# Attention scores of a pooled-attention and gated-MLP kernel: from one 128-row product for two heads to 64-row products for single heads, in turns on the two halves of TensorE

## The chip, the cores and the metric

The kernel runs on one core of a Trainium2 chip. The metric is the device time of one execution in microseconds (us). The median of three runs before the change is 771.92 us.

## What is computed

Pooled attention over 8 batches, 8 heads, 576 tokens and head size 64, and behind it a gated two-matrix product with two more matrices. All inputs are float32.

```python
k_p = k.reshape(B, H, Sp, pool, D).mean(axis=3)      # 576 keys -> 72 pooled keys
v_p = v.reshape(B, H, Sp, pool, D).mean(axis=3)
scores = scale * np.matmul(q, k_p.transpose(0, 1, 3, 2))
scores = scores - np.max(scores, axis=-1, keepdims=True)
attn = np.exp(scores)
attn = attn / (np.sum(attn, axis=-1, keepdims=True) + 1e-09)
attn_out = np.matmul(attn, v_p)
x = attn_out.transpose(0, 2, 1, 3).reshape(B * S, H * D)   # 4608 x 512
a = x @ w1; b = x @ w2                                     # 512 -> 1024
out = (a * b @ w3) @ w_out                                 # w3 @ w_out is made once
```

## The kernel before

The 4608 tokens are worked in 12 chunks of 384 tokens, numbered n (attention) or m (the products behind it) from 0 to 11. A chunk lies in one batch, or its two halves lie in two batches: a chunk with n % 3 == 1 is four token tiles of 96 tokens, any other is three tiles of 128. So the chunks 2 to 11 have 21 tiles of 128 tokens and 12 tiles of 96.

While the products of chunk m run, the attention of chunk m + 1 is worked out between them. The order of the work is written out by hand: every step is entered in a plan at a time slot (`at`), tables named SHIFT and LATER move single steps by fractions of a slot, and at the end the plan is sorted and the steps are issued in that order. Every engine works its own instructions strictly in that order. TensorE (PE) so gets one stream, in which the parts of the attention stand between the long products: `a_mm` and `b_mm` (12 passes of 384 columns each, line 676) and `out_mm` (9 passes of 512 columns, line 714).

The steps of one token tile t of chunk n, for n of 2 and more:

- `s_mm(n, t, half)` (line 449) makes the scores of four heads into one bank of PSUM. The queries `qT` lie as four pairs of heads, each pair on 128 partitions (64 for the even head, 64 for the odd one). The pooled keys `kbd` of a pair are block diagonal: 72 columns with the even head's keys on partitions 0 to 63 and zeros below, and 72 columns the other way round. One product over 128 rows so gives the scores of two heads, 144 columns. It is a float32 product, which the compiled program makes in two passes, each with a weight load of its own. Half 0 has the pairs 0 and 1 (heads 0 to 3), half 1 the pairs 2 and 3.
- `soft1` on VectorE (DVE): the extreme of each head (line 465) and the subtraction into `E` (line 469). After it the bank is free.
- `soft_e` on ScalarE (ACT): the exponential of all eight heads, once both halves are there (line 482). `soft_s` and `soft2` on VectorE: the sums and the division.
- `te_turn` transposes on VectorE (line 573), `te_out` and `te_in` send the result through DRAM, and `av_mm` (lines 647 to 650) multiplies with the pooled values on TensorE.

The pool `patt` has three banks (the name `att`) for all of the attention's products: scores, `av_mm`, and the transposes of pooled keys (line 358). Each new `att` takes the bank of the one three before it, and TensorE waits until that one has been read. The weights of a product (`lhsT`, here the queries) are loaded by an instruction of their own, which the profile lists as engine PEld.

Of the kernel before, what the change touches and what calls it, by code (L numbers as in the profile page):

```python
# [8 lines left out]
F32 = mybir.dt.float32  # L9
# [10 lines left out]
def kernel(  # L20
# [14 lines left out]
    nc = tc.nc  # L35
    ctx.enter_context(tc.manual_schedule())
    B, H, S, D = q.shape
    k_in = k
    P = 128
    POOL = 8  # L40
    KP = S // POOL
# [4 lines left out]
    NPR = H // 2  # L46
# [6 lines left out]
    NT = 2  # L53
# [20 lines left out]
    patt = ctx.enter_context(tc.tile_pool(name="patt", bufs=3, space=PSUM))  # L74
# [4 lines left out]
    kbd = [cp.tile([P, NPR, 2 * KP], F32, name=f"kbd{i}") for i in range(2)]  # L79
# [7 lines left out]
        out=msk,  # L87
# [173 lines left out]
    def pieces(n):  # L261
        i, r = divmod(n, 3)
        if r == 0:
            return [(2 * i, 0, 384, 0)]
        if r == 1:
            return [(2 * i, 384, 192, 0), (2 * i + 1, 0, 192, 192)]
        return [(2 * i + 1, 192, 384, 0)]

    def tok_tiles(n):
        res = []  # L270
        for (b, s0, cnt, off) in pieces(n):
            step = 128 if cnt == 384 else 96
            for x in range(0, cnt, step):
                res.append((b, off + x, step))
        return res
# [46 lines left out]
    qT = {}  # L322
# [119 lines left out]
    Sp = {}  # L442

    def s_mm(n, t, half):
        b, off, nt = tok_tiles(n)[t]
        ps = Sp[n, t, half] = patt.tile([P, 512], F32, tag="att", name="att")
        for j in range(2):
            pr = 2 * half + j
            nc.tensor.matmul(  # L449
                out=ps[:nt, 2 * KP * j:2 * KP * (j + 1)],  # L450
                lhsT=qT[n][:, pr, off:off + nt],
                rhs=kbd[b % 2][:, pr],
                start=True, stop=True,
            )

    def soft1(n, t, half):

        b, off, nt = tok_tiles(n)[t]
        if half == 0:
            Et[n, t] = p2.tile([P, H, KP], F32, tag="E", name="E")  # L460
            Mt[n, t] = [p2.tile([P, H], F32, tag=tag, name=tag) for tag in ("mx", "sm")]
        E, (mx, sm) = Et[n, t], Mt[n, t]
        hs = slice(4 * half, 4 * half + 4)
        sv = Sp.pop((n, t, half))[:nt, :4 * KP].rearrange("p (h k) -> p h k", k=KP)
        nc.vector.tensor_reduce(out=mx[:nt, hs], in_=sv, axis=AX.X, op=ALU.min)  # L465
        if (n, t) in SOFT_ACT:
            stage["sv", n, t, half] = sv
            return
        nc.vector.tensor_tensor(  # L469
            out=E[:nt, hs], in0=sv,  # L470
            in1=mx[:nt, hs].unsqueeze(2).broadcast_to([nt, 4, KP]), op=ALU.subtract)

    def soft_e(n, t, half):
        b, off, nt = tok_tiles(n)[t]
        E, (mx, sm) = Et[n, t], Mt[n, t]
        hs = slice(4 * half, 4 * half + 4)
        if (n, t) not in SOFT_ACT:
            if (n, t) not in HALF:
                if half == 0:
                    return  # L480
                hs = slice(0, H)
            nc.scalar.activation(out=E[:nt, hs], in_=E[:nt, hs], func=AF.Exp, scale=-1.0)  # L482
            return
        sv = stage.pop(("sv", n, t, half))
        for i in range(4):
            h = 4 * half + i
            nc.scalar.activation(  # L487
                out=E[:nt, h], in_=sv[:, i], func=AF.Exp, scale=-1.0, bias=mx[:nt, h:h + 1],
                accum_out=sm[:nt, h:h + 1])

    def soft_s(n, t, half):
        if (n, t) in SOFT_ACT:
            return
        b, off, nt = tok_tiles(n)[t]
        hs = slice(4 * half, 4 * half + 4)
        if (n, t) not in HALF:
            if half == 0:
                return
            hs = slice(0, H)
        nc.vector.reduce_sum(out=Mt[n, t][1][:nt, hs], in_=Et[n, t][:nt, hs], axis=AX.X)  # L500
# [247 lines left out]
    def W_lo(i):  # L748
# [59 lines left out]
        "prep_v": (2, 2, {(1, 0): -2.75, (1, 1): -2.75}),  # L808
        "prep_v3": (2, 2, {(0, 0): 2, (0, 1): 2}),
        "prep_vr": (2, 2, {(1,): -3}),  # L810
        "s_mm": (3, 2, {(0, 2, 1): -0.25, (1, 0, 0): -2.5, (1, 0, 1): -0.75, (1, 1, 0): -2.5, (1, 1, 1): -2.5, (1,
# [4 lines left out]
        "soft_e": (3, 2, {(0, 0, 0): 0.5, (0, 2, 1): -0.25, (1, 1, 1): -2.5, (1, 2, 0): -0.25, (1, 3, 1): -0.25, (2,  # L816
            2, 1): -1.75}),
        "soft_s": (3, 2, {(0, 0, 0): 0.5, (2, 1, 0): 0.5, (2, 2, 1): -1.75}),
        "te_turn": (3, 2, {(2, 2): -2.25}),
        "vr_hi": (2, 2, {(1,): -2.75}),  # L820
        "vr_sub": (2, 2, {(1,): -2.75}),
# [12 lines left out]
    def plan_att(n, s_at, ds, pt_at, av_at):  # L834


        for t in range(len(tok_tiles(n))):
            for half in range(2):
                k = s_at[t] + ds * half
                at("A", k, s_mm, n, t, half)  # L840
                at("P", k + 1, soft1, n, t, half)
                at("P", k + 1, soft_e, n, t, half)
                at("P", k + 1, soft_s, n, t, half)
            at("P", k + 2, soft2, n, t)
            if n >= NT:
                at("P", k + 3, te_turn, n, t)
                np_, ng, nx = split_of(n)
                if t % nx == nx - 1:
                    at("L", k + 4, te_out, n, t // nx)
                    at("L", k + 5, te_in, n, t // nx)  # L850
                continue
            at("P", k + 3, soft3, n, t)
            at("P", k + 3, soft4, n, t)
            k = pt_at[t]
            at("A", k, pt_mm, n, t)
            at("A", k, ptr_mm, n, t)
            at("P", k + 1, pt_post, n, t)
            at("P", k + 1, pt_lo, n, t)
            at("P", k + 1, ptr_post, n, t)
# [124 lines left out]
    for n in range(1, NCH):  # L984
        k = M0 + 3 * NJ * (n - 1)
        nt = len(tok_tiles(n))
# [48 lines left out]
```

## Time and profile before

| | |
|---|---|
| three runs, us | 770.85, 771.92, 772.44 (median 771.92) |
| the profiled execution: its own time, us | 771.39 |
| its span from the first to the last instruction, us | 769.5 |
| PE busy | 752.5 us, 98% |
| PEld (weight loads) busy | 698.6 us, 91% |
| DVE / ACT / POOL busy | 56% / 36% / 26% |
| granted TensorE clock over the span | 1.000 |

How to read it: 1.9 us of the profiled execution lie outside the span, and it is 0.5 us under the median. A PE that is 98% busy is not PE at its peak, because passes overlap in the pipeline and an interval counts as busy as soon as one of them is in it. The pace of a group of passes is read from the starts of neighbours, not from the length of one. "Passes" are the MATMUL records; each has one LDWEIGHTS record.

### The profile page before, as it was taken

Reading aid. Unit: us, or ns where it says so; the run is one execution under the profiler, and the core shown is the slowest. Engines: PE = TensorE matmul, PEld = TensorE weight load, DVE = VectorE, ACT = ScalarE, POOL = GpSimd, SP = SyncE. Lnnn points to the kernel's source line nnn. Section 1 sums busy time; section 2 is a strip of 40 time slices with the busy share of each in tenths; the row PEclk is TensorE's granted clock in tenths of the full one; section 3 lists DMA queues with packets and bytes.
Section 4 is the critical chain, followed back from the end, with each engine's and each line's share of the span. In section 5 each row is a group of like instructions: output and inputs, shape, how many; then the busy total and the mean of one; then the engine's idle time right before and its main releaser. Section 6 shows DMA issues by size and latency. Waiting matters only on the chain.

```text
span 769.5 us, 11333 instructions
## 1 busy us (share of the span) xinstructions
PE 752.5 (98%) x4154; PEld 698.6 (91%) x4154; DVE 433.9 (56%) x828; ACT 280.7 (36%) x638; POOL 197.8 (26%) x228
## 2 busy tenths in 40 slices
PE   7889999999999999999999999999999999999998
PEld 6667999999999999999999999999999999999997
DVE  5779987565555574555555563655545664643211
ACT  6768797213233232213323223213233233222211
POOL 3114284034325320024235320025144320000000
PEclk9999999999999999999999999999999999999999
DMA  9999970148134333138244323246244233130101
GB/s 329 295 206 218 267 150 0 40 117 155 53 112 90 82 99 72 64 101 150 70 114 73 99 79 72 72 115 126 73 122 87 75 97 54 42 108 1 41 1 42
DMA packets 121623, 80.12 MB, mean 104 GB/s; under 512 B 75488, under 2 KB 105376, under 8 KB 121568
## 3 DMA queue, kind: packets, MB, share of 16 engines
q1 hardware_dynamic: 121568, 79.40, 42.1%
q8 instruction: 33, 0.54, 0.3%
q14 instruction: 22, 0.18, 0.1%
HBM read 61.08 MB, written 18.28 MB: 103 GB/s over the span
## 4 chain that ended last, share of the span: by engine, by line
PE 81%; DMA 7%; DVE 6%; SPq 2%; ACT 2%; issue 1%; DVEq 0%; ACTq 0%
PE b L676 24%; PE a L676 23%; PE o L714 23%; DMA raw<-in_moe_w_dram 4%; PE att L449 4%; PE att L650 1%; DMA PTr<-D 1%; PE att L649 1%; PE att L648 1%; PE att L647 1%; PE o L740 1%; DVE E L510 1%; DMA D<-T 1%; DVE PTr L614 1%; ACT E L487 1%
## 5 line engine op out<-in xcount | busy, mean ns | idle before, releaser
L676 PE MATMUL b<-xT,hl 128*128 128x384 f32 x1152 | 219.1, 338 | 0.3 <-DVE a L696 0.2
L676 PE MATMUL a<-xT,hl 128*128 128x384 f32 x1152 | 219.1, 338 | 0.0
L676 PEld LDWEIGHTS a<-xT,hl 128*128 128x128 f32 x1152 | 203.4, 188 | 5.9
L676 PEld LDWEIGHTS b<-xT,hl 128*128 128x128 f32 x1152 | 199.7, 188 | 1.2 <-DVE a L696 0.9
L714 PE MATMUL o<-Wc,gh 128*128 128x512 f32 x576 | 182.7, 398 | 0.0
L696 DVE TENSOR_TENSOR a<-b,a 128x384 f32<-128x384 f32 x96 | 53.2, 554 | 166.1 <-PE b L676 165.4
L387 POOL TENSOR_TENSOR st<-st 72x512 f32<-72x512 f32 (+2 forms) x49 | 65.1, 1328 | 228.5 <-DMA st<-in_k_dram 156.2
L701 ACT CAST gh<-a 128x384 fp32r<-128x384 f32 x96 | 49.3, 513 | 199.5 <-DVE a L696 199.4
L714 PEld LDWEIGHTS o<-Wc,gh 128*128 128x128 f32 x576 | 105.5, 189 | 17.2
L714 PE MATMUL o<-Wc,gl 128*128 128x512 f32 x288 | 114.0, 396 | 0.0
L686 ACT COPY a<-a 128x384 f32<-128x384 f32 x96 | 46.0, 479 | 181.5 <-PE a L676 172.0
L705 DVE TENSOR_TENSOR gl<-a,gh 128x384 fp32r<-128x384 f32 x96 | 62.7, 653 | 20.4 <-ACT gh L701 19.5
L714 PEld LDWEIGHTS o<-Wc,gl 128*128 128x128 f32 x288 | 54.1, 188 | 12.6
L662 DVE TENSOR_TENSOR xT<-att,xT 128x384 fp32r<-128x384 f32 x48 | 26.6, 556 | 55.0 <-ACT xT L657 54.9
L449 PE MATMUL att<-kbd,qT 128*128 128x144 f32 (+1 forms) x320 | 50.3, 286 | 1.3 <-ACT E L487 1.3
L449 PEld LDWEIGHTS att<-kbd,qT 128*128 128x128 f32 (+1 forms) x320 | 46.0, 179 | 3.4 <-ACT E L487 1.5
L465 DVE TENSOR_REDUCE mx<-att 128x4 f32<-128x288 f32 (+1 forms) x80 | 35.3, 442 | 23.4 <-PE att L449 23.4
L388 POOL TENSOR_TENSOR st<-st 72x256 f32<-72x256 f32 (+2 forms) x49 | 44.5, 909 | 3.8
L482 ACT ACTIVATE E<-E 128x576 f32<-128x576 f32 (+2 forms) x35 | 23.5, 671 | 47.0 <-DVE E L469 47.0
L740 PE MATMUL o<-hl 128*128 128x512 f32 x144 | 38.0, 399 | 0.8 <-POOL hl L195 0.8
L500 DVE TENSOR_REDUCE sm<-E 128x8 f32<-128x576 f32 (+2 forms) x35 | 25.6, 730 | 23.2 <-ACT E L482 23.2
L423 POOL TENSOR_TENSOR st<-st,vrh 32x128 f32<-32x128 f32 x8 | 3.9, 485 | 123.8 <-ACT vrh L418 119.8
(104 smaller groups left out, 771.4 us busy)
## 6 DMA issues: line engine op xcount, KB each, us to landing
raw<-in_moe_w_dram SPq DMA_DIRECT2D x32, 512.0 KB
st<-in_k_dram SPq DMA_DIRECT2D x32, 288.0 KB
out_dram<-ob SPq DMA_DIRECT2D x35, 256.0 KB
st<-in_v_dram SPq DMA_DIRECT2D x32, 256.0 KB
qs<-in_q_dram SPq DMA_DIRECT2D x112, 48.0 KB
D<-T SPq DMA_DIRECT2D x7, 768.0 KB
PTl<-D SPq DMA_DIRECT2D x28, 192.0 KB
raw<-in_moe_w_out_dram SPq DMA_DIRECT2D x8, 512.0 KB
```

The lines of the kernel that those rows point to most:

```text
L387: eng.tensor_tensor(out=t[:, :, 0:4], in0=t[:, :, 0:4], in1=t[:, :, 4:8], op=ALU.add)
L388: eng.tensor_tensor(out=t[:, :, 0:2], in0=t[:, :, 0:2], in1=t[:, :, 2:4], op=ALU.add)
L449: nc.tensor.matmul(out=ps[:nt, 2 * KP * j:2 * KP * (j + 1)], lhsT=qT[n][:, pr, off:off + nt], rhs=kbd[b % 2][:, pr], start=True, stop=True,)
L465: nc.vector.tensor_reduce(out=mx[:nt, hs], in_=sv, axis=AX.X, op=ALU.min)
L662: nc.vector.tensor_tensor(out=xl, in0=ps, in1=f(xh), op=ALU.subtract)
L676: nc.tensor.matmul(out=o, lhsT=w12[j, w][sw][:, kt * P:(kt + 1) * P], rhs=x[sx][:, kt], start=(i == 0), stop=(i == 3 * NK - 1))
L686: nc.scalar.copy(out=a, in_=gt[m, j][:, :CH])
L696: nc.vector.tensor_tensor(out=g, in0=ps[:, :CH], in1=g, op=ALU.mult)
L701: nc.scalar.copy(out=gh, in_=g)
L705: nc.vector.tensor_tensor(out=gl, in0=g, in1=f(gh), op=ALU.subtract)
L714: nc.tensor.matmul(out=oacc[m][t], lhsT=(gh, gl)[sg][:, c], rhs=W[j][sw], start=(j == 0 and i == 0), stop=(j == NJ - 1 and i == 2))
L740: nc.tensor.matmul(out=wacc[h][it], lhsT=w3t[s][sa][:, it * P:(it + 1) * P], rhs=wo[j][sb], start=(j == 0 and i == 0), stop=(j == NJ - 1 a ...
```

## The change

For the chunks 2 to 11 the scores of a tile are no longer made in two calls of `s_mm` but in one (the call for half 1 returns at once). It takes two banks, one for the even heads and one for the odd heads. For each of the four pairs there are two products: one over the 64 partitions of the even head, with the 72 key columns of that head alone, and one over the other 64 partitions for the odd head. The zeros of `kbd` are not multiplied any more. A tile has 8 products of 72 columns over 64 rows instead of 4 of 144 columns over 128 rows. The later steps take every second head (`heads`) instead of the first or last four. The tables that place the steps have other numbers for `s_mm`, `soft1`, `soft_e`, `soft_s` and `soft2`.

```diff
     def s_mm(n, t, half):
         b, off, nt = tok_tiles(n)[t]
+        if n >= NT:
+            if half == 1:
+                return
+            for par in range(2):
+                Sp[n, t, par] = patt.tile([P, 512], F32, tag="att", name="att")
+            for pr in range(NPR):
+                for par in range(2):
+                    r = slice(64 * par, 64 * par + 64)
+                    nc.tensor.matmul(
+                        out=Sp[n, t, par][:nt, KP * pr:KP * (pr + 1)],
+                        lhsT=qT[n][r, pr, off:off + nt],
+                        rhs=kbd[b % 2][r, pr, KP * par:KP * (par + 1)],
+                        start=True, stop=True,
+                    )
+            return
         ps = Sp[n, t, half] = patt.tile([P, 512], F32, tag="att", name="att")
...
+    def heads(n, half):
+        return slice(4 * half, 4 * half + 4) if n < NT else slice(half, H, 2)
+
     def soft1(n, t, half):
...
-        hs = slice(4 * half, 4 * half + 4)
+        hs = heads(n, half)
...
-        "s_mm": (3, 2, {(0, 2, 1): -0.25, (1, 0, 0): -2.5, (1, 0, 1): -0.75, (1, 1, 0): -2.5, (1, 1, 1): -2.5, (1,
+        "s_mm": (3, 2, {(0, 0, 0): 1, (0, 1, 0): 1, (0, 2, 0): 0.75, (0, 2, 1): -0.25, (1, 0, 0): 0.25, (1, 0, 1):
```

What the order of TensorE's instructions is at one place, in chunk 5 (lines have other numbers after the change: 676 is 694, 714 is 732, 449 is 454 for the new products). Names are out<-moving,weights. Before, from the end of a `b_mm` to the next `a_mm`; the first half of tile 1 stands ahead of this `b_mm`:

```order
L676 MATMUL b<-xT_3244,hl 128x384
L676 MATMUL b<-xT_3243,hl 128x384
L449 MATMUL att<-kbd_85,qT 128x144 x4
L714 MATMUL o_3466<-Wc,gh 128x512 x2
L714 MATMUL o_3466<-Wc,gl 128x512
L714 MATMUL o_3467<-Wc,gh 128x512 x2
L714 MATMUL o_3467<-Wc,gl 128x512
L714 MATMUL o_3468<-Wc,gh 128x512 x2
L714 MATMUL o_3468<-Wc,gl 128x512
L449 MATMUL att<-kbd_85,qT 128x144 x2
L676 MATMUL a<-xT_3243,hl 128x384
```

and after:

```order
L694 MATMUL b<-xT_3284,hl 128x384
L694 MATMUL b<-xT_3283,hl 128x384
L454 MATMUL att<-kbd_85,qT 128x72 x8
L732 MATMUL o_3506<-Wc,gh 128x512 x2
L732 MATMUL o_3506<-Wc,gl 128x512
L732 MATMUL o_3507<-Wc,gh 128x512 x2
L732 MATMUL o_3507<-Wc,gl 128x512
L732 MATMUL o_3508<-Wc,gh 128x512 x2
L732 MATMUL o_3508<-Wc,gl 128x512
L454 MATMUL att<-kbd_85,qT 128x72 x8
L694 MATMUL a<-xT_3283,hl 128x384
```

The whole of tile 1 is now one group of 8 products, and the whole of tile 2 the next; before, four groups of two products each held the halves of both tiles (here the second half of tile 1 and the first of tile 2 stood together). Every tile of the chunks 2 to 11 has one such group, 33 groups in all, with long 128-row products ahead of and behind each.

VectorE at the same place, before, from the subtraction of tile 1's first half to the first half of tile 2:

```order
L469 TENSOR_TENSOR E<-att,mx 128x288
L696 TENSOR_TENSOR a<-b,a 128x384
L465 TENSOR_REDUCE mx<-att 128x4
L469 TENSOR_TENSOR E<-att,mx 128x288
L500 TENSOR_REDUCE sm<-E 128x8
L465 TENSOR_REDUCE mx<-att 128x4
L469 TENSOR_TENSOR E<-att,mx 128x288
```

and after:

```order
L714 TENSOR_TENSOR a<-b,a 128x384
L483 TENSOR_REDUCE mx<-att 128x4
L487 TENSOR_TENSOR E<-att,mx 128x4x72
L483 TENSOR_REDUCE mx<-att 128x4
L487 TENSOR_TENSOR E<-att,mx 128x4x72
L518 TENSOR_REDUCE sm<-E 128x8
L723 TENSOR_TENSOR gl<-a,gh 128x384
L483 TENSOR_REDUCE mx<-att 128x4
L487 TENSOR_TENSOR E<-att,mx 128x4x72
```

Both banks of tile 1 are now read one right after the other, behind the product a * b; the same operations stand there, with a subtraction that writes every second head.

## Rows read from the trace of the kernel before

**Rows 1.** The profile's page: busy time of each engine, and the granted TensorE clock in 40 slices of the span (9 is 90% or more).

```profile
span 769.5 us, 11333 instructions
...
PE 752.5 (98%) x4154; PEld 698.6 (91%) x4154; DVE 433.9 (56%) x828; ACT 280.7 (36%) x638; POOL 197.8 (26%) x228
...
PEclk9999999999999999999999999999999999999999
```

**Rows 2.** The page's chain of work that ended last, as shares of the span by engine.

```profile
PE 81%; DMA 7%; DVE 6%; SPq 2%; ACT 2%; issue 1%; DVEq 0%; ACTq 0%
```

**Rows 3.** Busy time of the engines in ten stretches from 150 to 720 us, in which the scores of the chunks 3 to 11 lie: length, then busy us and number of instructions of each engine. The last line is the sum.

```profile
310.00:370.00 60.00, 59.88 (x329) 56.08 (x329) 33.98 (x63) 16.27 (x32) 18.75 (x21) 1.00 0.43 101
...
sum 570.00, PE 568.57 PEld 534.14 DVE 314.60 ACT 164.38 POOL 146.06; mean PE 56.86 PEld 53.41 DVE 31.46 ACT 16.44 POOL 14.61
```

**Rows 4.** What TensorE waited for from 150 to 720 us: total us, times, longest.

```profile
PE att L650 <- DVE PTr L614: 1.1, 3, 0.5
PE b L676 <- DVE a L696: 0.2, 1, 0.2
```

**Rows 5.** The chain in order of time from 310 us (chunk 5): start, us, what, number of passes. Each pass counts from its start to that of the next.

```profile
311.02 0.09 PE att L647
311.11 0.11 PE att L648
311.22 0.11 PE att L649
311.33 0.11 PE att L650
...
311.88 2.11 PE o L714 x9
314.00 0.49 PE att L449 x4
314.49 2.08 PE a L676 x12
316.57 0.49 PE att L449 x4
317.06 2.11 PE b L676 x12
319.18 2.09 PE o L714 x9
321.27 2.11 PE a L676 x12
323.37 0.49 PE att L449 x4
```

**Rows 6.** Groups of passes and of weight loads over the whole span, shapes kept apart: line, engine, operation, out<-moving,weights, rows*weight columns, count, busy us, mean ns of one.

```profile
L449 PE MATMUL att<-kbd,qT 128*128 128x144 f32 x192 | 30.4, 287 | 1.3 <-ACT E L487 1.3
L449 PE MATMUL att<-kbd,qT 128*96 128x144 f32 x128 | 19.9, 286 | 0.0
...
L358 PE MATMUL att<-ident,km 72*128 72x72 f32 x32 | 3.4, 228 | 1.3 <-ACT qT L305 1.3
...
L449 PEld LDWEIGHTS att<-kbd,qT 128*128 128x128 f32 x192 | 28.3, 189 | 2.8 <-ACT E L487 1.5 <-DVE hl L213 0.2
...
L449 PEld LDWEIGHTS att<-kbd,qT 128*96 128x96 f32 x128 | 17.7, 162 | 0.6
...
L358 PEld LDWEIGHTS att<-ident,km 72*128 72x128 f32 x32 | 3.2, 141 | 1.9 <-ACT qT L305 1.7
```

**Rows 7.** The weight loads of eight `av_mm` passes of 192 columns, in order of time: start, us.

```profile
301.92 0.19 PEld L648 LDWEIGHTS att<-PTl,vbd 128*128 128x128 f32 x1
302.02 0.19 PEld L649 LDWEIGHTS att<-PTh,vbd 128*128 128x128 f32 x1
302.14 0.19 PEld L650 LDWEIGHTS att<-PTr,VR 128*128 128x128 f32 x1
...
302.58 0.19 PEld L650 LDWEIGHTS att<-PTr,VR 128*128 128x128 f32 x1
302.69 0.30 PEld L714 LDWEIGHTS o<-Wc,gh 128*128 128x128 f32 x2
```

**Rows 8.** The four transposes of pooled keys, 72 columns each, in order of time on PE: start, us from the first start to the last end, count.

```profile
194.03 0.42 PE L358 MATMUL att<-ident,km 72*128 72x72 f32 x4
```

**Rows 9.** VectorE and TensorE around a half of the scores, in order of time: start, us; in brackets idle time before.

```profile
314.53 0.46 DVE L465 TENSOR_REDUCE mx<-att 128x4 f32<-128x288 f32 x1 [0.47 <-PE att L449]
315.02 0.46 DVE L469 TENSOR_TENSOR E<-att,mx 128x288 f32<-128x288 f32 x1
...
323.21 0.65 PE L449 MATMUL att<-kbd,qT 128*128 128x144 f32 x4
...
324.73 0.42 DVE L465 TENSOR_REDUCE mx<-att 128x4 f32<-128x288 f32 x1
325.18 0.46 DVE L469 TENSOR_TENSOR E<-att,mx 128x288 f32<-128x288 f32 x1
```

More of the change, by code (lines that the diff above doesn't have):

```diff
@@ L475, in soft_e @@
         E, (mx, sm) = Et[n, t], Mt[n, t]
-        hs = slice(4 * half, 4 * half + 4)
+        hs = heads(n, half)
         if (n, t) not in SOFT_ACT:
@@ L494, in soft_s @@
         b, off, nt = tok_tiles(n)[t]
-        hs = slice(4 * half, 4 * half + 4)
+        hs = heads(n, half)
         if (n, t) not in HALF:
@@ L810 @@
         "prep_vr": (2, 2, {(1,): -3}),
-        "s_mm": (3, 2, {(0, 2, 1): -0.25, (1, 0, 0): -2.5, (1, 0, 1): -0.75, (1, 1, 0): -2.5, (1, 1, 1): -2.5, (1,
[4 rows of a table removed]
-        "soft_e": (3, 2, {(0, 0, 0): 0.5, (0, 2, 1): -0.25, (1, 1, 1): -2.5, (1, 2, 0): -0.25, (1, 3, 1): -0.25, (2,
-            2, 1): -1.75}),
-        "soft_s": (3, 2, {(0, 0, 0): 0.5, (2, 1, 0): 0.5, (2, 2, 1): -1.75}),
+        "s_mm": (3, 2, {(0, 0, 0): 1, (0, 1, 0): 1, (0, 2, 0): 0.75, (0, 2, 1): -0.25, (1, 0, 0): 0.25, (1, 0, 1):
[6 rows of a table added]
+        "soft_e": (3, 2, {(0, 0, 0): 1.25, (0, 0, 1): 0.25, (0, 1, 0): 1.25, (0, 1, 1): 0.25, (0, 2, 0): 1, (1, 0,
+            0): 0.5, (1, 1, 1): -2.25, (1, 3, 0): 1.25, (1, 3, 1): 0.25, (2, 0, 0): 0.25, (2, 1, 0): 1.25, (2, 1,
+            1): 0.25, (2, 2, 1): -1.75}),
+        "soft_s": (3, 2, {(0, 0, 0): 1.25, (0, 0, 1): 0.25, (0, 1, 0): 1.25, (0, 1, 1): 0.25, (0, 2, 0): 1, (1, 0,
+            0): 0.5, (1, 3, 0): 1.25, (1, 3, 1): 0.25, (2, 0, 0): 0.25, (2, 1, 0): 1.25, (2, 1, 1): 0.25, (2, 2, 1):
+            -1.75}),
         "te_turn": (3, 2, {(2, 2): -2.25}),
```

10 rows, old and new, of the table LATER are left out of this document.

## The prediction

> **What bounds the kernel now.** The page comes first: TensorE is busy in 98% of the span and its clock is at the full 2.4 GHz level in every slice [rows 1]; the chain that ended last is TensorE for 81%, the rest being mostly the load phase [rows 2]. Then the stretches where the changed scores lie: in 570 us TensorE is busy for 568.57, VectorE for 314.60 [rows 3], and what TensorE waited for there adds up to 1.3 us [rows 4]. So nothing but the length of TensorE's own stream counts in this part, and every microsecond that the scores gain or lose in that stream is a microsecond of the kernel, as long as no new wait comes up.
>
> The chain in order of time gives the pace of each kind of pass [rows 5]. Four score passes take 0.49 us, 0.122 each. Twelve passes of 384 columns take 2.08, 0.173 each; nine of 512 take 2.11, 0.234 each. A score pass is recorded as 0.287 long [rows 6], so 0.287 - 0.122 = 0.165 us of each lie in the pipeline under the next pass.
>
> **What is removed.** 33 tiles with 8 passes at 0.122 us: 0.98 us a tile, 32.2 us in all. This is paced by the 144 columns, at 0.122 / 144 a column: 0.85 ns.
>
> **What is added: 16 passes a tile, each of 72 columns, each with its own weight load.** The columns alone cost half of 0.122, 0.061 us a pass (the four 72-column transposes agree: 0.42 less the last one's 0.228, by three, is 0.064 [rows 8, 6]). So 16 passes that follow one another have the same column time as 8 before, and a gain comes only from the two halves of the array running at once.
>
> But a pass needs its weights, and there the number of loads doubles while the load stays 128 (or 96) columns wide. What a load needs is seen where it paces the stream. The `av_mm` passes have 192 columns, half of 384, and should follow each other at 0.087 us; the first does (0.09), the next at 0.11 [rows 5]. Their loads start from 301.92 to 302.69, seven steps in 0.77 us: 0.110 us a load of 128 columns [rows 7]. A load of 96 columns is recorded 0.027 shorter (162 ns against 189 [rows 6]), so I take 0.110 - 0.027 = 0.083. Before, this was hidden under a pass of 0.122; now it is longer than the pass of 0.061, and the loads set the pace. (The transposes' loads are cheaper, recorded at 141 ns [rows 6], and follow at 0.064. Their form is another; I keep it for the low end.)
>
> The order on TensorE is even head pass 1, pass 2, odd head pass 1, pass 2, next pair. With loads of the two halves side by side, and passes starting in order, one step of 0.110 holds the second pass of one half and the first pass of the other: even 1; even 2 with odd 1; odd 2 with even 3; and so on, nine steps for sixteen passes. If the first load hides under the product ahead, a tile costs 8 x 0.110 + 0.061 = 0.941 us, or 8 x 0.083 + 0.061 = 0.725 for 96 tokens. Against 0.976 (8 x 0.122) that is 0.035 less on each of 21 tiles and 0.251 less on each of 12: 0.7 + 3.0 = **3.7 us gained**, and this needs both overlaps and free changes between 128 and 64 rows.
>
> **What the changes of row mode cost.** Each of the 33 groups stands between long 128-row products, so the array changes from 128 rows to 64 and back 66 times. No row of before shows such a change: every product there is over 128 rows, or over 72 or 96 from partition 0, and none begins at partition 64. I bound it. Below: nothing. Above: the pipeline runs empty at each change (0.165 us, what a pass still has in it when the next starts [rows 6, 5]) and the load can't go ahead either (0.110): 0.275 us, 66 times, 18 us. I take the case in which the pipeline runs empty at each change and the load is exposed on one of the two sides: 2 x 0.165 + 0.110 = 0.44 us a group, or 0.41 at 96 tokens: 21 x 0.44 + 12 x 0.41 = 14.2 us. The reason is that a pass over 128 rows uses both halves, so neither half can take another kind of pass while it is in there.
>
> The Trainium skill, "TensorEngine Tiling (Array Packing)", Key Properties, says that a change of tiling mode drains TensorE, while separate tiles may load weights and multiply in parallel. By that rule both choices above hold; no run so far shows either.
>
> **Sum.** -3.7 + 14.2 = +10.5 us on a span of 769.5, so 780 us. The profiled execution is 771.39 against a median of 771.92, so I add to the median: **782.4 us**. With free loads (2 x 0.165 alone, 33 times 0.33) it is -3.7 + 10.9 = +7.2; with loads exposed at every change +14.4 (18 less 3.7). The likeliest case's own range is so 776 to 788, some microseconds wider for the unknown empty-pipeline time.
>
> **Costed at nothing.** VectorE's work is the same in number and elements; the subtraction that writes every second head is 0.46 us in rows of 288 contiguous elements [rows 9]; should the steps cost it something, VectorE has 255 of 570 us free [rows 3] behind TensorE. The two banks at once: a tile's second bank is the one that the tile before it had as its first, and in seven chunks two tiles stand only 2.1 us apart (2, 5, 8 and 11: nine 512-column passes, 2.11; 4, 7 and 10: twelve of 384, 2.08 [rows 5]). VectorE frees a bank at 315.02 + 0.46 = 315.48 for passes that began at 314.00, 1.5 us, and when it is late at 325.64 for 323.37, 2.3 us, with the 0.49 us of the passes themselves in both [rows 9, 5]; so the bank is free 1.0 to 1.8 after the passes, under 2.1. In the new order the a * b product is ahead of the score reads, but its input ends before the scores do. If VectorE were 1 us late at all seven places it would be some 5 to 7 us, since everything on TensorE queues behind that wait; by the rows a margin of 0.3 us stands. The softmax behind it starts no later: both halves are complete together, and before, the exponential waited for the second half.
>
> **Rivals.**
> 1. *Faster: the changes of mode are free, the halves overlap.* -3.7 us, at most -5.9 (eight steps instead of nine: 21 x 0.096 + 12 x 0.312 = 5.8): 766 to 768. For it: the same queue runs loads ahead of passes everywhere now [rows 5, 7]. Against it: the 128-row pass lies in both halves for 0.165 us after its last column. It decides at 0.06 us a change (3.7 / 66): above that the kernel is not faster.
> 2. *Loads one after another.* If only one load runs at a time, sixteen loads take 1.76 us (1.33): +0.784 x 21 + 0.352 x 12 = 16.5 + 4.2 = +20.7 us with free changes of mode, **792.6**, and some 800 to 807 with them. The change would then not do what it says: the halves take turns, but not at once. For it: in every row of before the loads of neighbours start at least one pace apart [rows 7], though there all of them go to the same 128 rows.
> 3. *The halves run fully side by side and loads do not pace.* Nine steps of 0.061: 0.549 us a tile, 0.427 less, 33 times: -14.1 us, **757.8**. For it: the transposes' loads at 0.064 [rows 8]. Against it: the score loads are recorded at 189 ns like those of `av_mm`, not at 141 [rows 6]. The Trainium skill, "TensorE: Matmul & The Clock Gate", Part 3, gives the span of packed products as one product's length and about 4 ns for each further tile, with 3.07 times for four 32-row tiles of 512 columns; with that the scores would about halve. What it measured is 512 columns to a load, and the trace here has 72.
> 4. *Cheap changes* (about 0.04 to 0.08 us each) cancel the gain: within 1.5 us of before.
>
> **How the numbers follow.** The forecast 0.36 (776 to 790). Rival 2 0.30 (788 to 808). Rival 1 0.18, rival 3 0.06, rival 4 0.10. The range 764 to 801 leaves out rival 3 and the upper half of rival 2 with its 66 changes, under 0.2 together. A difference under 0.2% (1.5 us) is about what a measurement of this kernel can't tell from none. Faster: 0.18 + 0.06 = 0.24. Same: 0.10. Slower: 0.36 + 0.30 = 0.66.
>
> **What would show it.** In the profile after: 528 score passes in place of 264 for these chunks. In the chain of a group, sixteen passes with two starts close together for each 0.110 us where the halves overlap, and with 0.110 between every two where they don't (rival 2). At the change from 128 to 64 rows, a first score pass that starts about 0.4 us after the last long pass instead of 0.23, and the same behind the group. TensorE's waits for `att` banks should stay at about 1 us; a line "PE att <- DVE E" with several us would mean that the bank margin was wrong. Groups of the 96-token tiles shorter than those of 128 by about 0.2 us would show that loads pace; equal ones that columns or the issue of instructions do. The prediction is wrong if a group costs less than 0.98 us from the last pass ahead to the first pass behind.

## The result, and the profile after

The changed kernel takes 779.59 us (median of four runs, 777.44 to 780.85) against 772.18 for the kernel before: a ratio of 1.0095, with a 95% interval from 1.0068 to 1.0122. It is 7.4 us slower. The profiled execution took 780.85 us and is the longest of the four; its span grew by 9.5 us, from 769.5 to 779.0.

The page after, with the lines that answer to [rows 1] and [rows 2]:

```profile
span 779.0 us, 11870 instructions
...
PE 760.4 (98%) x4418; PEld 695.5 (89%) x4418; DVE 431.2 (55%) x828; ACT 280.2 (36%) x638; POOL 195.7 (25%) x228
...
PE 82%; DVE 8%; DMA 6%; ACT 2%; SPq 1%; issue 1%; POOL 0%; DVEq 0%; ACTq 0%
```

TensorE is still the bound. It has 264 more passes and as many more loads, and VectorE's share of the chain has risen from 6 to 8%.

The score passes after, and their weight loads, to be held against [rows 6]: line, engine, operation, out<-moving,weights, rows*columns, count, busy us, mean ns.

```profile
L454 PE MATMUL att<-kbd,qT 64*128 64x72 f32 x336 | 23.4, 279 | 0.0
L454 PE MATMUL att<-kbd,qT 64*96 64x72 f32 x192 | 10.8, 252 | 0.0
```

```profile
L454 PEld LDWEIGHTS att<-kbd,qT 64*128 64x128 f32 x336 | 20.4, 188 | 5.7 <-issue 5.7
L454 PEld LDWEIGHTS att<-kbd,qT 64*96 64x96 f32 x192 | 9.1, 161 | 3.3 <-issue 3.3
```

A group at 128 tokens is busy for 23.4 / 21 = 1.11 us, one at 96 tokens for 10.8 / 12 = 0.90, although both have the same columns. The load unit now stands idle ahead of the groups, (5.7 + 3.3) / 33 = 0.27 us each; in [rows 6] the loads ahead of the scores had hardly any idle time (2.8 and 0.6 us before all 320 of them, the load phase included).

One group in the order of time, tile 0 of chunk 5, in the windows around it (the same passes appear in more than one row, with as many as the window touches): first TensorE, then its loads.

```profile
318.93 0.34 PE L694 MATMUL a<-xT,hl 128*128 128x384 f32 x1
319.20 0.33 PE L454 MATMUL att<-kbd,qT 64*128 64x72 f32 x2
...
319.20 1.11 PE L454 MATMUL att<-kbd,qT 64*128 64x72 f32 x16
320.25 0.45 PE L694 MATMUL b<-xT,hl 128*128 128x384 f32 x1
...
320.25 0.62 PE L694 MATMUL b<-xT,hl 128*128 128x384 f32 x2
```

```profile
318.76 0.19 PEld L694 LDWEIGHTS a<-xT,hl 128*128 128x128 f32 x1
...
319.20 0.19 PEld L454 LDWEIGHTS att<-kbd,qT 64*128 64x128 f32 x2 [0.25 <-issue]
```

Two passes start together and two loads start together. The last pass of `a` ahead of them starts at 318.93, and the first score pass 0.27 later instead of 0.17; its load starts no earlier than the pass itself. Behind the group the second pass of `b` ends its record at 320.25 + 0.62; with the usual 0.34 of a pass it starts at 320.53, 0.28 after the first instead of 0.17. Read from start to start, and with the usual pace of the long passes on both sides taken off, every one of the 21 groups of 128 tokens takes 1.25 us, and every one of the 12 of 96 tokens 1.04 us (they agree within 0.01). Before, it was 0.98 for both. So the groups cost 21 x 0.274 + 12 x 0.06 = **6.5 us**.

The rest is in new waits of TensorE. From 143 us to 715 us, the answer to [rows 4]:

```profile
PE att L668 <- DVE PTr L632: 2.5, 3, 1.1
PE b L694 <- DVE a L714: 1.8, 3, 0.9
```

Added up from the starts of the long passes (each gap over the usual pace by more than 0.13 us) TensorE waited 5.6 us in this part, against 2.6 in the kernel before: **3.0 us**. (The view gives less, 4.3 and 1.3, because it counts only the time in which no pass is on record.) 6.5 and 3.0 are the 9.5 us of this execution. The medians are only 7.4 us apart, which leaves about 0.9 us beside the groups if these cost the same each time; so the 3.0 us of waits are those of this one, long execution.

The wait for a * b at chunk 5, on VectorE and on TensorE (in brackets idle time before):

```profile
337.18 0.46 DVE L487 TENSOR_TENSOR E<-att,mx 128x288 f32<-128x288 f32 x1
...
339.06 0.70 DVE L591 STREAM_TRANSPOSE T<-E 128x512 f32<-128x512 f32 x1
...
340.21 0.76 DVE L528 TENSOR_TENSOR E<-E,sm 128x576 f32<-128x576 f32 x1
341.00 0.71 DVE L591 STREAM_TRANSPOSE T<-E 128x512 f32<-128x512 f32 x1
...
341.76 0.52 DVE L714 TENSOR_TENSOR a<-b,a 128x384 f32<-128x384 f32 x1
```

```profile
337.47 0.62 PE L732 MATMUL o<-Wc,gh 128*128 128x512 f32 x2
...
339.56 2.27 PE L694 MATMUL a<-xT,hl 128*128 128x384 f32 x12
342.33 0.98 PE L694 MATMUL b<-xT,hl 128*128 128x384 f32 x4 [0.49 <-DVE a L714]
```

The product a * b reads the bank `b` and has had its input since about the time at which the nine `out_mm` passes ahead of 339.56 began. It stands behind the transposes and the division of the last two tiles in VectorE's order, and the next `b_mm` waits for that bank.

In the kernel before it stands behind the same operations. The same place there:

```profile
332.87 0.46 DVE L469 TENSOR_TENSOR E<-att,mx 128x288 f32<-128x288 f32 x1
...
337.46 0.52 DVE L696 TENSOR_TENSOR a<-b,a 128x384 f32<-128x384 f32 x1
```

```profile
333.54 0.62 PE L714 MATMUL o<-Wc,gh 128*128 128x512 f32 x2
```

From the end of the last read of a score bank to a * b it is 4.1 us in both kernels (333.33 to 337.46, and 337.64 to 341.76). What has moved is that read: it ends 0.2 us before the `out_mm` passes begin in the kernel before, and 0.2 us after their start in the changed one. In the chunks 2 and 8 it ends 1.2 and 0.3 us later than before, counted from the last pass of `b_mm`.

### The profile page after: what moved, and what is told of

It reads as the page before. It is cut to its first block, busy times and chain, and to the rows that moved or that the text cites. A ratio compares the mean times of both kernels' runs of the same rounds, so it can differ in the third digit from the quotient of the medians.

```text
span 779.0 us, 11870 instructions
## 1 busy us (share of the span) xinstructions
PE 760.4 (98%) x4418; PEld 695.5 (89%) x4418; DVE 431.2 (55%) x828; ACT 280.2 (36%) x638; POOL 195.7 (25%) x228
## 4 chain that ended last, share of the span: by engine, by line
PE 82%; DVE 8%; DMA 6%; ACT 2%; SPq 1%; issue 1%; POOL 0%; DVEq 0%; ACTq 0%
PE b L694 23%; PE o L732 22%; PE a L694 22%; PE att L454 4%; PE o L758 3%; DMA raw<-in_moe_w_dram 2%; PE att L668 1%; DMA D<-T 1%; DVE E L528 1%; DMA PTr<-D 1%; PE att L667 1%; PE att L666 1%; PE att L665 1%; DMA raw<-in_moe_w_out_dram 1%; DVE E L487 1%; DVE sm L518 1%
## 5 line engine op out<-in xcount | busy, mean ns | idle before, releaser
L723 DVE TENSOR_TENSOR gl<-a,gh 128x384 fp32r<-128x384 f32 x96 | 59.5, 620 | 20.3 <-ACT gh L719 19.5
L388 POOL TENSOR_TENSOR st<-st 72x256 f32<-72x256 f32 (+2 forms) x49 | 41.5, 847 | 3.8
L454 PEld LDWEIGHTS att<-kbd,qT 64*128 64x128 f32 (+1 forms) x528 | 29.5, 178 | 9.0 <-issue 9.0
L454 PE MATMUL att<-kbd,qT 64*128 64x72 f32 (+1 forms) x528 | 34.2, 269 | 0.0
```

The source lines that it names most:

```text
L388: eng.tensor_tensor(out=t[:, :, 0:2], in0=t[:, :, 0:2], in1=t[:, :, 2:4], op=ALU.add)
L454: nc.tensor.matmul(out=Sp[n, t, par][:nt, KP * pr:KP * (pr + 1)], lhsT=qT[n][r, pr, off:off + nt], rhs=kbd[b % 2][r, pr, KP * par:KP * (pa ...
L723: nc.vector.tensor_tensor(out=gl, in0=g, in1=f(gh), op=ALU.subtract)
```

## The experiments

Every kernel changes one thing in the changed kernel, except where it says otherwise. The two right columns of the table at the end are worked out from the starts of passes in each run's trace, as above.

**1. All products over 128 rows.** No change of row mode and nothing side by side.

```diff
-                    r = slice(64 * par, 64 * par + 64)
+                    r = slice(0, P)
```

> The changed kernel with all eight products of a tile over the whole 128 rows (72 columns each; the block diagonal's zeros make the result the same). No change of row mode, nothing side by side. If weight loads pace passes on the same rows: 16 x 0.112 = 1.79 us a tile of 128 tokens and 16 x 0.085 = 1.36 at 96, against 0.98 before: +17.0 + 4.6 = +21.6 us, and about 3 us of waits as in the changed kernel: 796 to 797 us. If the columns pace and loads are hidden: 16 x 0.061 = 0.98, 772 to 776 us.

792.78 us, 1.0265 (1.0235 to 1.0295).

**2. All products on the lower 64 rows.** Change of mode, nothing side by side; the scores of the odd heads are left out.

```diff
-                    r = slice(64 * par, 64 * par + 64)
+                    r = slice(0, 64)
```

> The changed kernel with all eight products of a tile on the lower 64 rows (the odd heads are left out: their products meet the zeros of the block diagonal). Changes of row mode as in the changed kernel, nothing side by side. If a change of mode itself costs what the changed kernel's trace shows around its groups (about 0.34 us in and out together): 33 x 0.34 = 11 us above the kernel with full rows, some 807 us, with the same 0.095 and 0.11 us on both sides of a group. If the cost around a group comes from having two halves (or two banks) at work, and not from the mode: the same as full rows, 796 us, and passes in a group 0.112 and 0.085 apart in both cases.

805.19 us, 1.0429 (1.0394 to 1.0464). The score passes of the first and then of the second of these kernels:

```profile
L454 PE MATMUL att<-kbd,qT 128*128 128x72 f32 x336 | 39.9, 272 | 0.0
L454 PE MATMUL att<-kbd,qT 128*96 128x72 f32 x192 | 18.0, 247 | 0.0
```

```profile
L454 PE MATMUL att<-kbd,qT 64*128 64x72 f32 x336 | 42.0, 275 | 0.0
L454 PE MATMUL att<-kbd,qT 64*96 64x72 f32 x192 | 18.9, 248 | 0.0
```

Over 128 rows a group takes 39.9 / 21 = 1.90 us of busy time and 18.0 / 12 = 1.50, and from start to start 1.79 and 1.39: sixteen steps of 0.112 and 0.087. So passes on the same rows follow each other at the pace of the loads, and not at the 0.061 of the columns. (The time is 3 us under what was expected, and this trace has no more waits than the kernel before, where 3 us were expected.) On one half, with changes of mode, the group takes 2.14 and 1.71, which is 0.35 and 0.32 more, and the two kernels differ by 12.4 us, 0.38 for each of 33 groups. With both halves at work the group takes 1.25 and 1.04. So the overlap does halve the sixteen steps (0.89 us less at 128 tokens). But eight steps, 0.90 us at 128 tokens and 0.69 at 96, are only 0.08 and 0.29 less than the 0.98 of the four wide products, because those were paced by their columns and hid their loads; and the change of mode, 0.35, is more than either.

**3. Even heads first, then odd heads**, the same products in another order.

```diff
-            for pr in range(NPR):
-                for par in range(2):
+            for par in range(2):
+                for pr in range(NPR):
```

> The changed kernel with the same products in another order: the four even heads first, then the four odd heads. If passes start in the program's order, or TensorE looks only a few instructions ahead, the halves hardly overlap: 16 steps in place of 8, 8 x 0.112 x 21 + 8 x 0.085 x 12 = 27 us more than the changed kernel, some 806 us. If each half has its own queue that is at least eight passes deep: the same 779.6 us, with two passes 0.007 us apart at each step.

793.87 us, 1.027 (1.023 to 1.031): between both. (The profiled execution, 788.50 us, is the shortest of the four.)

```profile
L454 PE MATMUL att<-kbd,qT 64*128 64x72 f32 x336 | 33.9, 279 | 0.0
L454 PE MATMUL att<-kbd,qT 64*96 64x72 f32 x192 | 15.6, 252 | 0.0
```

A group takes 1.75 us from start to start; less the 0.35 of the two changes, that is 12.5 steps of 0.112, where 8 would be full overlap and 16 none. In the program all eight even passes stand ahead of the first odd one, so some odd passes run beside even ones that stand well ahead of them in the program. In the first group of this trace passes start 0.112 apart (the first step is 0.17) until the fifth, a sixth starts together with the fifth, and two interleaved rows follow; the other 32 groups have the first pair at the same place. The records don't name the half, so I read the second row as the odd heads. Then the first odd pass starts ahead of three even ones that stand before it in the program, and it didn't start while four or more were waiting; what sets this limit no run shows. Neither theory was right; turns of one head each, as in the change, are near enough for full overlap.

**4. The old products in the new order**: one group a tile, two banks at once, the new tables, and four products of 144 columns over 128 rows, with heads 0 to 3 in one bank and 4 to 7 in the other.

```diff
-            for pr in range(NPR):
-                for par in range(2):
-                    r = slice(64 * par, 64 * par + 64)
+            for par in range(2):
+                for j in range(2):
                     nc.tensor.matmul(
-                        out=Sp[n, t, par][:nt, KP * pr:KP * (pr + 1)],
-                        lhsT=qT[n][r, pr, off:off + nt],
-                        rhs=kbd[b % 2][r, pr, KP * par:KP * (par + 1)],
+                        out=Sp[n, t, par][:nt, 2 * KP * j:2 * KP * (j + 1)],
+                        lhsT=qT[n][:, 2 * par + j, off:off + nt],
+                        rhs=kbd[b % 2][:, 2 * par + j],
...
-        return slice(4 * half, 4 * half + 4) if n < NT else slice(half, H, 2)
+        return slice(4 * half, 4 * half + 4)
```

> The changed kernel's order (one group a tile, two banks at once, the new tables), with the old products of 144 columns over 128 rows and the old split of the heads over the banks. No change of row mode. If the 3.0 us of the loss that don't lie in the score groups are waits that the new order makes: 775 us, with TensorE's waits behind a * b and behind PTr at about 4 us in all. If those waits come only because the groups are longer: as before, 772 us, waits at about 1.5 us.

772.16 us, 0.9997 (0.9977 to 1.0017): the new order alone costs nothing in time. Its waits are another mixture, though:

```profile
PE b L693 <- DVE a L713: 2.1, 3, 0.9
```

The wait behind a * b (2.6 us counted from the starts, at the same three places as in the changed kernel, against 0.6 before) comes with the new order, without any of the new products. The order alone doesn't make it, though: in experiments 1, 2 and 3, where the same order stands beside longer groups, it is 0.2, 0 and 0. The wait behind PTr, 2.0 us in the kernel before, is 0.4 here, so the sum is almost unchanged.

**5. One 128-row pass more in each group**, a transpose of the identity into an unused part of the bank: in the middle of the group, where it makes the array leave 64 rows and come back, and as a control at its end.

```diff
             for pr in range(NPR):
+                if pr == 2:
+                    nc.tensor.transpose(out=Sp[n, t, 0][:, 384:512], in_=ident, identity=ident)
                 for par in range(2):
```

> The changed kernel with one 128-row transpose of the identity (128 columns, into an unused part of the bank) after the fourth product of each group, so that the array leaves 64 rows and comes back once more in each of the 33 groups. If each pair of changes costs about 0.34 us: 33 x (0.34 + 0.11 for the pass itself) = 15 us above the changed kernel, some 794 us. If a change of mode costs nothing and the loss around a group is of another kind: 33 x 0.11 = 3.6 us, 783 us.

> The control: the same transpose after the eighth product, where the array leaves 64 rows anyway. Every theory: the pass itself, 33 x 0.11 = 3.6 us above the changed kernel, 783 us. A little less if its cheaper weight load (about 0.06 us against 0.11) is the one that is exposed behind the change in place of the long product's: 33 x 0.06 = 2 us, 781 us.

791.64 us (1.0263, 1.0216 to 1.031) and 781.26 us (1.0139, 1.01 to 1.0178). The difference is 10.4 us, 0.31 for each of the 33 extra pairs of changes; from start to start the groups are 0.35 longer. The chain of the kernel with the pass in the middle, around a group, and the same of the control:

```profile
319.32 2.11 PE a L696 x12
321.43 0.60 PE att L456 x8
322.03 0.26 PE att L453
322.29 0.60 PE att L456 x8
322.89 2.28 PE b L696 x12
```

```profile
322.54 1.04 PE att L454 x16
323.59 0.26 PE att L460
323.85 2.09 PE b L695 x12
```

From the first score pass to the end of `b` it is 3.74 us with the pass in the middle and 3.39 in the control, and the transpose stands in both. So it is the change of mode that costs, wherever it stands, and not the border to the long products.

**6. Twice the columns**, 144 in each product (72 of them zeros, put where the next product overwrites them).

```diff
-            for pr in range(NPR):
+            for i in range(NPR):
...
+                    pr = (i, NPR - 1 - i)[par]
...
-                        out=Sp[n, t, par][:nt, KP * pr:KP * (pr + 1)],
+                        out=Sp[n, t, par][:nt, KP * pr:KP * (pr + 2)],
...
-                        rhs=kbd[b % 2][r, pr, KP * par:KP * (par + 1)],
+                        rhs=kbd[b % 2][r, pr],
...
+        c0 = KP if n >= NT and half == 1 else 0
```

> The changed kernel with each product over all 144 columns of the pair (72 of them zeros, put where the next product overwrites them): twice the columns, same loads, same mode, same halves. If loads pace the steps: 0.122 for the columns in place of 0.112 and 0.085: 21 x 8 x 0.010 + 12 x 8 x 0.037 = 1.7 + 3.6 = +5.2 us, 785 us, and groups of 96 and of 128 tokens become equally long. If columns pace them: 8 x 0.061 more a tile, 33 times: +16 us, 796 us.

787.38 us, 1.0211 (1.0175 to 1.0247).

```profile
L455 PE MATMUL att<-kbd,qT 64*128 64x144 f32 x336 | 26.3, 296 | 0.0
L455 PE MATMUL att<-kbd,qT 64*96 64x144 f32 x192 | 14.7, 292 | 0.0
```

With twice the columns a group of 128 tokens grows by only (26.3 - 23.4) / 21 = 0.14 us, one of 96 by (14.7 - 10.8) / 12 = 0.33, and both are now busy for 1.23 to 1.25. Inside a group the steps are 0.123 us at 128 and at 96 tokens, as their columns say; in the changed kernel they are 0.112 and 0.085, with half the columns. So there it is the loads that pace, as forecast. Only the first step of a group is longer than forecast, 0.23 and 0.20 us in place of 0.17 and 0.14, which no run here explains.

**7. a * b earlier** in VectorE's order, in the chunks 2, 5, 8 and 11.

```diff
-        "soft2": (3, 2, {(0, 0): 0.25, (0, 1): 0.25, (1, 3): 0.25, (2, 1): 0.25, (2, 2): -1.75}),
+        "soft2": (3, 2, {(0, 0): 0.25, (0, 1): 0.25, (1, 3): 0.25, (2, 1): 0.25, (2, 2): -0.75}),
-        "te_turn": (3, 2, {(2, 2): -2.25}),
+        "te_turn": (3, 2, {(2, 1): 1, (2, 2): -1.25}),
```

> The changed kernel with one other order on VectorE in the chunks 2, 5, 8 and 11: the product a * b, for which TensorE waits, ahead of the transposes and the division of the last two tiles instead of behind them; TensorE's order is the same. If these waits of 0.6 to 1.0 us each are part of the loss: 2 us less than the changed kernel, 777.5 us, and no wait of b behind a * b. If other waits take their place (the transposes, and so the way through DRAM, are about 1 us later): the same 779.6 us, with the wait behind PTr grown by as much.

777.04 us, 1.0065 (1.0039 to 1.0092). That is lower than the changed kernel's 1.0095, but the intervals overlap, so the reading rests on the trace. It has no wait of TensorE behind a * b any more, and 0.15 us of waits in all. The chain through chunk 5, to be held against [rows 5]:

```profile
322.86 2.09 PE o L732 x9
324.95 2.11 PE a L694 x12
327.06 2.08 PE b L694 x12
329.14 1.04 PE att L454 x16
330.19 2.30 PE o L732 x9
332.49 1.04 PE att L454 x16
```

TensorE runs through, and what stays is the price of the groups. The waits behind PTr were gone as well, which this edit doesn't explain. They lie between 0.1 and 4.0 us in the traces here, kernels with the same order there included, and single traces don't show what sets them.

**8 and 9. The same edit with the old products**: in the new order (the kernel of experiment 4 with the edit of experiment 7), and in the kernel before itself, whose diff this is.

```diff
-        "soft2": (3, 2, {(2, 2): -1.75}),
+        "soft2": (3, 2, {(2, 2): -0.75}),
-        "te_turn": (3, 2, {(2, 2): -2.25}),
+        "te_turn": (3, 2, {(2, 1): 1, (2, 2): -1.25}),
```

> The old 128-row products in the changed kernel's order (as the run of old products in the new order), and the product a * b ahead of the transposes and the division of the last two tiles (as in the run before this one). If the waits of b behind a * b, 2.6 us in the run of old products in the new order, are all that this order costs: they go, 769.6 us, and it is 0.3% under the kernel before. If the time won is lost at the next wait (PTr, or the banks of the scores): 772 us.

> The kernel before, with a * b ahead of the same transposes and division. There TensorE waits 0.62 us for a * b in all. If only this wait counts: 0.6 us less, 771.5, which can't be told from none. If the later transposes delay the attention's results: a wait behind PTr or the transfers, and 772 us or more.

769.40 us (0.9962, 0.9938 to 0.9986) and 769.69 us (0.9954, 0.9937 to 0.9972): both under the kernel before, by 2.6 to 2.9 us. In both traces TensorE no longer waits behind a * b. The waits there account for 1.0 to 1.1 us only (2.6 us before, 1.5 and 1.6 now), and the spans of the profiled executions (769.1 and 768.8 us) are only 0.4 and 0.7 under the 769.5 of the kernel before; the rest of the gain is not explained by these traces.

All runs together: the 33 score groups from start to start, and TensorE's waits from 143 us to the last chunk, both from the profiled execution of each kernel.

| kernel | time, us | groups, us | waits, us |
|---|---|---|---|
| before | 772.2 | 32.3 | 2.6 |
| changed | 779.6 | 38.7 | 5.6 |
| all over 128 rows | 792.8 | 54.2 | 2.5 |
| all on the lower half | 805.2 | 65.4 | 4.0 |
| even heads first | 793.9 | 53.8 | 0.4 |
| old products, new order | 772.2 | 32.3 | 2.9 |
| 128-row pass in the middle | 791.6 | 52.2 | 2.3 |
| 128-row pass at the end | 781.3 | 40.7 | 6.0 |
| 144 columns | 787.4 | 45.2 | 4.3 |
| a * b earlier | 777.0 | 38.7 | 0.1 |
| old products, new order, a * b earlier | 769.4 | 32.3 | 1.5 |
| before, a * b earlier | 769.7 | 32.3 | 1.6 |

In each row the time is that of before plus what groups and waits have grown, within 3 us.

## Why the prediction came out

It forecast +10.5 us (782.4) and the kernel is 7.4 us slower; the mechanism that it named is the one the runs show. Point by point:

- **The bound** held: what the scores gain or lose on TensorE is the kernel's.
- **Loads pace the steps** (0.110 and 0.083 us) held: 0.112 and 0.087 in experiment 1, the changed kernel's groups are 0.21 us shorter at 96 tokens than at 128, and experiment 6 shows it from the other side. Rival 3, in which columns pace, is out.
- **The halves run side by side** held: starts in pairs, and 1.25 us a group where one half alone takes 2.14. Rival 2, loads one after another, is out.
- **Nine steps** was wrong in its reason. I let passes start in the program's order, so that a second even pass and a first odd one share a step. Two passes start together from the first, and experiment 3 shows passes of one half running beside passes of the other that stand ahead of them. So what stands above on the kernel before, that every engine works its instructions strictly in order, doesn't hold for the starts of TensorE's passes. It is eight steps; the ninth, for which I put 0.061, doesn't exist.
- **The price of the changes of mode** was a little too high: 0.44 us a group forecast, 0.35 measured in three ways (0.35 and 0.32 in experiments 1 and 2, 0.35 in experiment 5, and 1.25 - 8 x 0.112 = 0.35 in the changed kernel). Of the 0.35, 0.095 lies ahead of the group: the first score pass and its load start at 319.20, 0.07 before the record of the last `a` pass ends, so the 0.165 that I took from the lengths of records was too much. 0.11 lies in the first long pass behind the group, whose record is 0.45 long instead of 0.34, and the other 0.15 in the group's first step and behind its last. I read these as the pipeline running empty twice, one whole load exposed and about half of another; no run separates them. The rule of the Trainium skill, "TensorEngine Tiling (Array Packing)", Key Properties, that a change of mode drains the array while separate tiles load and multiply in parallel, agrees with all of this; its price, which the page doesn't give, is here 0.35 us for a change and back. Rival 1, free changes, is out, and so is rival 4, cheap ones.
- **What I costed at nothing** was the step that failed. For VectorE's new order I checked only the banks of the scores, and there no wait came up; the subtraction that writes every second head takes 0.46 us, as before. I also wrote that the softmax starts no later. In the chunks 2, 5 and 8 it does: the last read of the scores ends 0.3 to 1.2 us later against TensorE's stream, and the exponential, the sums, the transposes and the division of two tiles that follow it, 4.1 us in both kernels, stand ahead of a * b, for which TensorE waits. That wait rose from 0.6 to 2.3 us, and experiment 4 shows that it comes with the order. The wait behind PTr rose from 2.0 to 3.3 in the profiled execution; its cause stays open.

The groups cost 6.5 us instead of 10.5, and the waits 3.0 in the profiled execution instead of none. So the two errors went opposite ways, and that the time came out as close as it did is partly luck. That the range covered both signs was right for what could be known: the sign hung on whether a single change costs less than 0.06 us or more, no row of before showed one, and it is about 0.17 (half of 0.35).

## What to carry to other kernels

Before a product is cut into smaller ones for halves of the array, look at what paces a pass: columns or the weight load. Here the cut halved the columns of a pass and left its load as wide as it was, so that the sixteen passes on two halves came out only 0.08 us under the four wide products at 128 tokens and 0.29 under at 96; and the switch of row modes and back in a stream of long products cost about a third of the group. By these numbers (an estimate; no run has longer groups) a group would have to be more than four times as long to pay at 128 tokens, and 1.2 times at 96. And when a change comes with a new order, go through everything that the engine which feeds the bound has to do, not only what the change touches: the wait that could be taken away was behind a product that had its input and stood too far back in the queue. It could be taken away in the kernel before as well, without the change: experiment 9 is 2.6 us under it, though its trace explains only part of that.

## What the runs showed of the hardware that I had not expected

- Passes on the two halves don't start in the program's order. With eight passes of one half ahead of the first of the other, 3.5 of 8 steps still overlapped (experiment 3); with two ahead, all did (the changed kernel).
- Two loads into the two halves start together (two within the 0.19 us of one, in the rows above), each as long as a load over 128 rows (188 ns against 189 in [rows 6]).
- A change from 128 rows to 64 and back costs 0.35 us, also around a single short pass (experiment 5). Around groups of 144-column passes it comes to about 0.40 at 128 tokens (experiment 6: 1.38 us from start to start, less eight steps of 0.123).
